# Another order of 879 operations in a transformer block on one core, with the last tile's output in 288 and 160 columns

## The chip, the cores and the metric

The kernel runs on one core of a Trainium2 chip. The metric is device microseconds of one execution. Beside it stands the profile of one further execution, whose span goes from the first to the last instruction. The engines are TensorE (PE; its weight loads are PEld), VectorE (DVE), ScalarE (ACT), GpSimd (POOL) and SyncE (SP), which here issues all DMA transfers.

## The reference

An attention layer with a sliding, dilated window, then a mixer and a two-layer product with gelu. S = 2048 rows, D = 448, F = 1792, 16 heads of 28, bf16.

```python
qkv = layernorm(x) @ wqkv                      # q, k, v
idx = pos[:, None] - arange(8) * 2             # 8 keys, every second row back
logits = einsum("bhsd,bhswd->bhsw", q, kg) * scale
p = softmax(where(mask, logits, -1e9)); o = einsum("bhsw,bhswd->bhsd", p, vg)
h = x + o @ wo
y = layernorm(h)
g = gelu(layernorm(y) @ w1)
x1 = y + shifted(g) @ w2                       # four column groups, shifted by 1 and 2 rows both ways
out = h + x1 + gelu(layernorm(x1) @ w3) @ w4
```

This is its shortened form; a layernorm subtracts the mean and divides by the square root of the variance plus 1e-5.

## The kernel before

All data stays in SBUF between the first load and the last store. The rows are worked in four stages t = 0 to 3 of 512 rows up to the hidden layer g, then in five units u = 0 to 4 of 2, 4, 4, 4 and 2 tiles of 128 rows. In the names below, the last digit is the stage or the unit.

- **N1, A1, V**: layernorm of x (N1), its turn into columns, the products for q and k (A1) and for v (V). Stages 0 and 1 are turned by TensorE with an identity, stages 2 and 3 by a DMA transpose from `lntm` to `actT`. V's results go to `vt`; DMA transfers copy them into windows, `vw` (four pieces a stage: vwp 16 rows of the stage before, vwa 64 rows, vwb 80 rows, vwc 16 rows of three tiles).
- **A2, S, A3, O**: VectorE multiplies q by shifted k (4096 elements a partition), TensorE sums the products with `zc`; the softmax (S); VectorE spreads the weights over `bd_r`, TensorE multiplies them with `vw` (A3: four groups of 32 small matmuls); O multiplies by wo and adds the residual.
- **B1, M**: layernorm of the sum and its DMA transpose (`actT`), product with w1 and gelu (M). B10 to B13 and M0 to M3 are its four stages. ACT's squares with running sums give the variance, ACT or POOL its power.
- **B2, T, W3, B3**, by unit: product of the shifted g with w2 (B2; from unit 2 on with rows gathered by small `ht` DMAs), layernorm and transpose (T), product with w3 and gelu to `h3T` (W3), product with w4, sum on VectorE and the output DMA (B3). Unit 4 is worked tile by tile.

A contraction of 448 is split over the upper and the lower 64 rows of TensorE: `duo` works two outputs as a **pair**, a first half (upper rows for one output, lower rows for the other) and a second half that swaps them and waits until the first is done.

What sets the order of the work is one list, `ORDER`, of 879 operation numbers. The phases are generated first, each operation with its number; `arrange` (line 192) then hands each engine its operations in the list's order, gives out the buffers of the pools in that order, and adds the waits. `OTHER` names the copies that go to their other engine (ACT to VectorE or back). A further rule stands in `arrange`: a DMA transpose waits for all loads and vw transfers ahead of it in the list, and those behind it wait for the transpose:

```python
if op.insts[0][0] == "dma_start_transpose":
    op.deps.update(turned + moved)
    turned, moved = [op], []
elif op.is_dma and not callable(op.chan):
    op.deps.update(turned)
    moved.append(op)
```

So the place of a load on SP decides which transposes it holds up and which hold it up. All instructions are recorded by one helper at line 1009 (1010 in the changed kernel), so that a profile's row is told apart by its tiles and shapes. Many copies from PSUM (`copy` in `phase_A1`, `phase_V`, the softmax and A3) may run on ACT or VectorE.

Of the kernel before, what the change touches and what calls it, by code (L numbers as in the profile page):

```python
# [15 lines left out]
NQK, NBD, NLN, NACT, NSM, NO = 3, 2, 2, 4, 1, 6  # L16
POWER = {'N1': 'aaaa', 'B1': 'aaaa', 'B2': 'apapp'}
RESIDUAL = 'ttvv'
ORDER = """
# [30 lines left out]
"""  # L50
OTHER = """
182 438 482 483 546 552
"""
FULL = (4,)
FILL = (0, 0, 0, 0)
# [226 lines left out]
def bass_sequential_preLN__sliding_local_dilated__mixer_s_mlp__prompt_kernel(  # L282
    nc, A_x, A_wqkv, A_wo, B_x, B_w1, B_w2, B_w3, B_w4, out,
):
    _, SEQ, D = A_x.shape
# [4 lines left out]
    NTL = SEQ // 128  # L290
# [22 lines left out]
    with ExitStack() as es:  # L313
# [87 lines left out]
        def dve(meth, block=False, **kw):  # L401
            op = S.add("dve", meth, **kw)
            op.block = block
            return op
# [4 lines left out]
        def dma(chan, out_ap, in_ap, nbytes, eng="sp", **kw):  # L409
            return S.add(eng, "dma_start", chan=chan, nbytes=nbytes, out=out_ap, in_=in_ap, **kw)  # L410
# [379 lines left out]
        def phase_A3(t):  # L790
# [14 lines left out]
            S.tag = "O%d" % t  # L805
            on_pe = RESIDUAL[t] == "t"
            summed = STATS["B1"][t] == "a"
# [59 lines left out]
        def phase_B2(u):  # L867
            tiles = UNITS[u]
            summed = STATS["B2"][u] == "a"
            dense = u >= 2  # L870
            n, first = 128 * len(tiles), 128 * tiles[0]
            if dense:
                for c, lo, hi, k, at in LOWER:
                    dma("ht", ht[at:at + hi - lo, k, 0:n], gT[lo:hi, c, 2 + first + SHIFT[c]:2 + first + SHIFT[c] + n], (hi - lo) * n * 2)

            def group(i, upper):
                b = _Tile(P_bank)

                def side(part, chunks):
                    return [(gT[part, c, 2 + i * 128 + SHIFT[c]:130 + i * 128 + SHIFT[c]], (lambda lo, m, c=c: w2_s[part, c, lo:lo + m])) for c in chunks]  # L880

                if dense:
                    top = side(TOP, range(3 + upper))
                    bot = [(ht[BOT, k, 128 * i - first:128 * i - first + 128], (lambda lo, m, k=k: w2_l[BOT, k, lo:lo + m])) for k in range(4 - upper)]
                else:
                    top, bot = side(TOP, range(4)), side(slice(64, KC), range(4))

                def out():
                    kw = dict(accum_out=mv[:, 2, i, 0:1]) if summed else {}
                    dve("scalar_tensor_tensor", out=xb[i], in0=xin[:, i, :], scalar=rs_y[:, 1, 0, i:i + 1], in1=b(lambda v: v[:, 0:D]), op0=ALU.mult, op1=ALU.add, **kw)  # L890
                    if not summed:
                        ln_stats(2, xb[i], i)

                return (lambda lo, n: b(lambda v: v[:, lo:lo + n]), top, bot), out

            for i in tiles[::2]:
                (A, out_a), (B, out_b) = group(i, True), group(i + 1, False)
                duo(A, B, ((0, D),))
                out_a()
                out_b()  # L900
            ln = _Tile(P_ln)
            if summed:
                sums_stats(2, tiles, lambda i: xb[i], ln)
            S.tag = "T%d" % u
            norms = norms_of("B2", u, len(tiles))
            rstd(2, tiles[0], len(tiles), summed, norms, POWER["B2"][u])
            last = [normalize(2, i, ln, n, xb[i], TURN["B2"][u], summed, norms[n]) for n, i in enumerate(tiles)]
            for i in tiles:
                S.add("pool", "tensor_tensor", after=last, out=xb[i], in0=xb[i], in1=xin[:, i, :], op=ALU.add).block = True
            b2_a[u] = transposed(ln, TURN["B2"][u], len(tiles))  # L910
# [20 lines left out]
        def phase_B3(u):  # L931
# [19 lines left out]
            else:  # L951
                for k, i in enumerate(UNITS[u]):
                    o = _Tile(P_o)
                    for n, (lo, m) in enumerate(((0, D // 2), (D // 2, D // 2)) if i == NTL - 1 else ((0, D),)):
                        b = _Tile(P_bank)
                        for first in range(0, NF, 7):
                            mms([(b(lambda v, m=m: v[:, 0:m]), h3[u][f](lambda v, k=k: v[:, k * 128:(k + 1) * 128]), w4_s[:, f, lo:lo + m],
                                  f == 0, f == NF - 1, m, None) for f in range(first, first + 7)])
                        store(i, b, o, lo, m, n)
# [27 lines left out]

        order = S.arrange([int(k) for k in ORDER.split()], [int(k) for k in OTHER.split()])
        _LAST["S"] = S; _LAST["order"] = order
# [61 lines left out]
```

## Time and profile before

| | us |
|---|---|
| median of 3 runs | 192.13 (191.79 to 192.33) |
| profiled execution | 191.2 |
| its span | 189.5 |
| TensorE busy | 180.3 |
| VectorE busy | 125.7 |
| ACT busy | 120.4 |
| POOL busy | 25.0 |

The span is the time from the first to the last instruction; the execution's own time is 1.7 us longer. TensorE's rows are matmuls, whose ends are modelled, so neighbours overlap. A releaser in brackets is what an engine waited for last.

### The profile page before, as it was taken

To read this page: it belongs to the slowest core of one execution; us is meant where nothing else is said; L and a number is where in the kernel's file an instruction comes from. 1 tells how busy PE (TensorE), PEld (TensorE's weight loads), DVE (VectorE), ACT (ScalarE), POOL (GpSimd) and SP (SyncE) were. 2 spreads that over 40 slices of the span, in tenths; PEclk is the share of its full clock that TensorE was granted. 3 is DMA by queue.
4 is the path that set the end of the run, shared out by engine and by line. 5 is a ranking of instruction groups with operands and counts; after the bars stand their busy time and mean duration, and the time that the engine had idled before them with its cause. 6 is when DMAs were issued, how large, how long until landed. Compare 5 with 4: busy or idle time off the path is not lost.

```text
span 189.5 us, 5776 instructions
## 1 busy us (share of the span) xinstructions
PE 180.3 (95%) x2496; PEld 93.8 (49%) x2496; DVE 125.7 (66%) x223; ACT 120.4 (64%) x289; POOL 25.0 (13%) x59
## 2 busy tenths in 40 slices
PE   6899998997999999999997999999999999999994
PEld 2474343443544574665444545554444544455773
DVE  6789899998999999989647437852086066000502
ACT  3659999887999999966794697232806004640250
POOL 3320000000000000244300000074002103900000
PEclk9999999999999999999999999999999999999999
DMA  5960045692654669902532210463300602300121
GB/s 133 362 207 0 9 93 138 162 203 46 127 125 90 129 201 378 249 13 38 147 71 50 58 35 3 96 76 91 118 24 7 114 0 73 83 0 0 52 73 48
DMA packets 33633, 18.59 MB, mean 98 GB/s; under 512 B 21336, under 2 KB 33096, under 8 KB 33608
## 3 DMA queue, kind: packets, MB, share of 16 engines
q1 hardware_dynamic: 33608, 18.23, 38.8%
q8 instruction: 19, 0.31, 0.7%
q14 instruction: 6, 0.05, 0.1%
HBM read 8.14 MB, written 1.84 MB: 53 GB/s over the span
## 4 chain that ended last, share of the span: by engine, by line
PE 66%; DMA 12%; DVE 10%; ACT 8%; POOL 1%; issue 1%; SPq 1%
PE ps L1009 66%; DMA actT<-lntm 5%; DMA vw<-vt 4%; ACT arena L1009 4%; DVE lntm L1009 3%; ACT actT L1009 2%; DVE st L1009 2%; DMA xin<-in_A_x_dram 2%; ACT lntm L1009 1%; POOL rs_y L1009 1%; DMA ht<-arena 1%; DVE arena L1009 1%; DVE qk_r L1009 1%; DVE xin L1009 1%; SPq L1009 1%
## 5 line engine op out<-in xcount | busy, mean ns | idle before, releaser
L1009 PE MATMUL ps<-actT,arena 64*128 64x512 bf16 (+2 forms) x812 | 70.4, 326 | 1.3 <-DMA actT<-lntm 0.6
L1009 ACT ACTIVATE h3T<-ps 128x512 bf16<-128x512 f32 (+1 forms) x70 | 30.5, 524 | 35.5 <-PE ps L1009 35.3
L1009 PEld LDWEIGHTS ps<-actT,arena 64*128 64x128 bf16 (+1 forms) x812 | 34.8, 96 | 33.0 <-PE ps L1009 1.7
L1009 PE MATMUL ps<-arena,h3T 64*128 64x448 bf16 (+2 forms) x434 | 44.5, 343 | 0.0
L1009 ACT ACTIVATE arena<-ps 128x512 bf16<-128x512 f32 (+6 forms) x64 | 29.5, 504 | 10.4 <-PE ps L1009 9.9
L1009 DVE SCALAR_TENSOR_TENSOR qk_r<-ps,mrs,arena 128x448 bf16<-128x448 f32 (+1 forms) x17 | 10.6, 651 | 33.9 <-PE ps L1009 18.5
L1009 DVE TENSOR_TENSOR qk_r<-arena 128x4096 bf16<-128x4096 bf16 (+1 forms) x16 | 31.9, 2014 | 0.7 <-PE ps L1009 0.7
L1009 PEld LDWEIGHTS ps<-arena,h3T 64*128 64x128 bf16 (+1 forms) x434 | 22.8, 94 | 19.2 <-ACT h3T L1009 0.2
L1009 POOL TENSOR_TENSOR arena<-arena,xin 128x448 f32<-128x448 f32 x16 | 16.2, 1033 | 54.2 <-DVE lntm L1009 38.5
L1009 DVE TENSOR_TENSOR bd_r<-arena,bmask 80x2048 bf16<-80x2048 bf16 x16 | 19.1, 1212 | 3.6 <-PE ps L1009 3.4
L1009 DVE SCALAR_TENSOR_TENSOR arena<-xin,rs_y,ps 128x448 f32<-128x448 bf16 x16 | 10.1, 674 | 8.5 <-PE ps L1009 8.5
L1009 ACT ACTIVATE actT<-ps 128x512 bf16<-128x512 f32 (+2 forms) x23 | 13.9, 636 | 2.1 <-PE ps L1009 1.9
L1009 PE MATMUL ps<-actT,w_s 64*112 64x512 bf16 x112 | 13.9, 379 | 1.3 <-DMA actT<-lntm 1.2
L1009 PE MATMUL ps<-wo_s,actT 64*128 64x448 bf16 x128 | 14.3, 350 | 0.4 <-ACT vt L1009 0.4
L1009 PE MATMUL ps<-arena,actT 64*128 64x448 bf16 x112 | 12.9, 350 | 0.1
L1009 PE MATMUL ps<-w_s,arena 64*128 64x448 bf16 x83 | 12.4, 349 | 0.5 <-DMA ht<-arena 0.5
L1009 ACT ACTIVATE lntm<-xin,nm 128x448 bf16<-128x448 bf16 x16 | 10.5, 658 | 2.1 <-DVE nm L1009 2.0
L1009 PEld LDWEIGHTS ps<-actT,w_s 64*112 64x112 bf16 x112 | 7.6, 126 | 6.2 <-DVE bd_r L1009 1.7
L1009 ACT ACTIVATE rs_x<-mv,epsilon 128x4 f32<-128x4 f32 (+2 forms) x16 | 4.4, 292 | 9.3 <-DVE mv L1009 9.2
L1009 DVE BATCH_NORM_STATS2 st<-xin 128x6 f32<-128x448 bf16 x16 | 9.0, 614 | 1.1 <-DMA xin<-in_A_x_dram 1.0
L1009 DVE TENSOR_SCALAR lntm<-arena,mv,rs_y 128x512 bf16<-128x512 f32 x14 | 6.8, 543 | 3.5 <-POOL rs_y L1009 2.9
L1009 PEld LDWEIGHTS ps<-w_s,arena 64*128 64x128 bf16 x83 | 5.7, 95 | 6.3 <-DMA ht<-arena 1.2
(72 smaller groups left out, 157.9 us busy)
## 6 DMA issues: line engine op xcount, KB each, us to landing
arena<-in_B_w_dram SPq DMA_DIRECT2D x2, 896.0 KB, 7.1
out_dram<-qk_r SPq DMA_DIRECT2D x15, 112.0 KB, 1.8
arena<-in_B_w_dram SPq DMA_DIRECT2D x2, 784.0 KB, 8.9
vw<-vt SPq DMA_DIRECT2D x4, 320.0 KB, 3.8
vw<-vt SPq DMA_DIRECT2D x4, 256.0 KB, 6.3
arena<-in_A_wqkv_dram SPq DMA_DIRECT2D x2, 448.0 KB, 4.5
xin<-in_A_x_dram SPq DMA_DIRECT2D x2, 448.0 KB, 7.0
xin<-in_A_x_dram SPq DMA_DIRECT2D x3, 224.0 KB, 5.3
```

What stands on the lines that cost most here:

```text
L1009: inst = getattr(eng, meth)(**kw)
```

## The change

`ORDER` is another list. `OTHER` goes from {182, 438, 482, 483, 546, 552} to {92, 182, 483, 489, 492, 495, 546, 552}: the copies 92 (A1 of stage 0) and 489, 492, 495 (A3 of stage 3) go from ACT to VectorE, 438 (A1 of stage 3) and 482 (softmax of stage 3) go back to ACT. `DENSE` names the unit from which `ht` is used, 2 as before. The last tile's output is worked in 288 and 160 columns, not 224 and 224.

```diff
+DENSE = 2
 ORDER = """
-2 0 8 1 29 7 9 11 39 10 40 33 12 13 36 14 15 16 30 17 18 41 19 42 31 43 32 50 55 56 20 51 6 52 62 37 44 45 57 58 53 60
...
+8 9 2 10 12 0 1 39 40 41 42 43 44 45 46 47 48 49 13 5 14 4 15 16 6 33 7 50 17 18 29 51 36 37 34 30 52 55 53 54 56 62
...
 OTHER = """
-182 438 482 483 546 552
+92 182 483 489 492 495 546 552
 """
...
-            dense = u >= 2
+            dense = u >= DENSE
...
-                    for n, (lo, m) in enumerate(((0, D // 2), (D // 2, D // 2)) if i == NTL - 1 else ((0, D),)):
+                    for n, (lo, m) in enumerate(((0, 288), (288, 160)) if i == NTL - 1 else ((0, D),)):
```

SP in the first quarter, before: behind the loads of x and wqkv, from wo's second load to the second DMA transpose (A13). `wo_s` is wo, `w_s` is w1 (two halves) and w2; the first four vw pieces after the first transpose are V0's and one of V1.

```order
L1009 DMA_TRANSPOSE actT<-lntm 128x16x128
L1009 DMA wo_s<-in_A_wo_dram 28x4x448 x2
L1009 DMA vw<-vt 80x4x512
L1009 DMA vw<-vt 64x4x512
L1009 DMA vw<-vt 16x3x512 x2
L1009 DMA wo_s<-in_A_wo_dram 28x4x448
L1009 DMA w_s<-in_B_w_dram 128x2x448 x2
L1009 DMA w_s<-in_B_w_dram 112x4x448
L1009 DMA vw<-vt 80x4x512
L1009 DMA vw<-vt 64x4x512
L1009 DMA_TRANSPOSE actT<-lntm 128x16x128
```

The same place after, up to the second transpose; `arena` from `in_B_w` 128x2x1792 is the first half of w3.

```order
L1010 DMA wo_s<-in_A_wo_dram 28x4x448 x4
L1010 DMA w_s<-in_B_w_dram 128x2x448 x2
L1010 DMA w_s<-in_B_w_dram 112x4x448
L1010 DMA_TRANSPOSE actT<-lntm 128x16x128
L1010 DMA vw<-vt 80x4x512
L1010 DMA vw<-vt 16x3x512
L1010 DMA vw<-vt 64x4x512
L1010 DMA vw<-vt 16x512
L1010 DMA vw<-vt 64x4x512
L1010 DMA vw<-vt 16x3x512
L1010 DMA vw<-vt 80x4x512
L1010 DMA arena<-in_B_w_dram 128x2x1792
```

The weights wo, w1 and w2 moved ahead of the first transpose, the vw pieces of V0 and V1 follow it without a load between them, and half of w3 stands ahead of the second transpose.

SP a little later, before: the pieces of V2 behind the second transpose (A13), the transposes of B10 and B11, then w3 and the first piece of V3.

```order
L1009 DMA vw<-vt 64x4x512
L1009 DMA vw<-vt 16x3x512
L1009 DMA vw<-vt 80x4x512
L1009 DMA vw<-vt 16x512
L1009 DMA_TRANSPOSE actT<-lntm 128x16x128 x2
L1009 DMA arena<-in_B_w_dram 128x2x1792 x2
L1009 DMA vw<-vt 16x512
```

The same place after:

```order
L1010 DMA vw<-vt 80x4x512
L1010 DMA vw<-vt 64x4x512
L1010 DMA vw<-vt 16x512
L1010 DMA_TRANSPOSE actT<-lntm 128x16x128 x2
L1010 DMA arena<-in_B_w_dram 128x2x1792
L1010 DMA vw<-vt 16x3x512
```

V2's piece of 16 rows of three tiles moved behind both transposes and behind the second half of w3.

TensorE from the end of O2 to M2, before. `wo_s` is O2, `arena,h3T` is B30 (the product with w4), `actT,arena` of 512 columns is W31, `ident,pb` the turn of the softmax's weights, `actT,w_s` M2 and `bd_r,vw` A33.

```order
L1009 MATMUL ps<-wo_s,actT 128x448 x8
L1009 MATMUL ps<-arena,h3T 128x448 x14
L1009 MATMUL ps<-wo_s,actT 128x448 x8
L1009 MATMUL ps<-arena,h3T 128x448 x28
L1009 MATMUL ps<-actT,arena 128x512 x58
L1009 MATMUL ps<-ident,pb 80x64 x16
L1009 MATMUL ps<-actT,arena 128x512 x20
L1009 MATMUL ps<-actT,w_s 112x512 x22
```

The same place after:

```order
L1010 MATMUL ps<-wo_s,actT 128x448 x8
L1010 MATMUL ps<-arena,h3T 128x448 x56
L1010 MATMUL ps<-actT,arena 128x512 x38
L1010 MATMUL ps<-ident,pb 80x64 x16
L1010 MATMUL ps<-actT,arena 128x512 x18
L1010 MATMUL ps<-actT,w_s 112x512 x22
L1010 MATMUL ps<-bd_r,vw 32x64 x64
L1010 MATMUL ps<-actT,w_s 112x512 x6
```

The whole of O2 now stands ahead of B30, and 22 of W31's matmuls moved from ahead of M2 to behind it.

58 rows, old and new, of the table ORDER are left out of this document.

## The prediction

> **What bounds the kernel now.** I read four things in this order: the page's totals and slices, the busy time by stretch, the list of what each engine waited for, and the chain of work that ended last. First the totals and the forty slices of the span:
>
> ```profile
> PE 180.3 (95%) x2496; PEld 93.8 (49%) x2496; DVE 125.7 (66%) x223; ACT 120.4 (64%) x289; POOL 25.0 (13%) x59
> PE   6899998997999999999997999999999999999994
> DVE  6789899998999999989647437852086066000502
> PEclk9999999999999999999999999999999999999999
> DMA  5960045692654669902532210463300602300121
> ```
>
> TensorE is busy 180.3 of 189.5 us, at the full granted clock in every slice. Its last 17 slices hold no gap, so whatever can be won lies earlier. VectorE's 66% is an average that hides the point: it is full up to slice 17 and half idle later. Busy time by stretch (us, then busy time and instructions of PE, PEld, DVE, ACT, POOL) says it in numbers:
>
> ```profile
> 8.12:130.00 121.88, 117.47 (x1871) 60.93 (x1873) 101.78 (x169) 96.61 (x236) 15.15 (x36) 1.00 0.47 113
> 130.00:186.67 56.67, 56.67 (x601) 30.42 (x596) 17.62 (x37) 19.85 (x44) 7.75 (x8) 1.00 0.19 49
> 13.00:85.00 72.00, 69.38 (x1181) 34.64 (x1181) 69.14 (x94) 66.47 (x170) 3.20 (x4) 1.00 0.52 129
> ```
>
> From 130 us on TensorE is busy 56.67 of 56.67. From 8.12 us (its first matmul with data) to 130 it is idle 121.88 - 117.47 = 4.4 us. From 13 to 85 us VectorE is busy 69.14 of 72.00, as full as TensorE (69.38): a stall taken from TensorE there is only worth what VectorE can follow. The waits of TensorE:
>
> ```profile
> PE ps L1009 <- DMA actT<-lntm: 1.8, 2, 1.2
> PE ps L1009 <- DMA vw<-vt: 1.0, 1, 1.0
> PE ps L1009 <- DMA ht<-arena: 0.5, 1, 0.5
> PE ps L1009 <- ACT vt L1009: 0.4, 1, 0.4
> ```
>
> These four are 3.7 of the 4.4 us. The timeline of TensorE has each of them, with the idle time and its releaser in brackets:
>
> ```profile
> 29.59 1.27 PE L1009 MATMUL ps<-actT,arena 64*128 64x512 bf16 x12 [0.64 <-DMA actT<-lntm]
> 42.52 0.74 PE L1009 MATMUL ps<-wo_s,actT 64*128 64x448 bf16 x6 [0.41 <-ACT vt L1009]
> 46.02 0.42 PE L1009 MATMUL ps<-bd_r,vw 80*32 80x64 bf16 x32 [0.99 <-DMA vw<-vt]
> 102.74 1.07 PE L1009 MATMUL ps<-actT,w_s 64*112 64x512 bf16 x8 [1.20 <-DMA actT<-lntm]
> 113.12 0.36 PE L1009 MATMUL ps<-w_s,arena 64*128 64x448 bf16 x1 [0.46 <-DMA ht<-arena]
> ```
>
> The chain (start, duration, what) shows what stood behind them:
>
> ```profile
> 25.10 4.35 DMA actT<-lntm
> ...
> 37.73 8.25 DMA vw<-vt
> ...
> 46.02 31.07 PE ps L1009 x506
> ...
> 77.11 0.42 DVE actT L1009
> ...
> 83.03 1.94 POOL rs_y L1009
> ...
> 91.89 2.73 ACT lntm L1009 x8
> ...
> 95.25 1.38 DVE lntm L1009 x4
> ...
> 96.66 5.94 DMA actT<-lntm
> ...
> 102.74 6.31 PE ps L1009 x170
> ...
> 126.14 60.81 PE ps L1009 x636
> ...
> 186.97 0.45 DVE qk_r L1009
> ```
>
> From 77 to 97 us the end is set by VectorE, POOL and ACT (layernorm B12), then by the transpose that M2 waits for. So M2's first matmul, 102.74 us, is the gate to everything behind it.
>
> **The change, part by part.** TensorE's own work is the same (2496 matmuls of the same shapes but for the last tile), so the sum is over waits.
>
> (a) The loads of wo, w1 and w2 leave before the first DMA transpose instead of behind it, with no vw transfer queued behind them. In before the vw of V1 waited behind w1 and w2 and took 8.25 us; the vw transfers of this trace in all:
>
> ```profile
> L1009 SPq DMA_DIRECT2D vw<-vt x15: 627/690/2394, 19.5 to 102.6; - x15
> DMA to landing us min/median/max: 2.2/3.9/8.5
> ```
>
> With the median 3.9 us the vw of V1, issued by about 35 us, is there by 39, seven us before it is wanted at 46: the wait of 0.99 goes. What hides the loads, issued from 7 us on behind x, is the stretch of 14 to 24 us: the DMA row has 0 in slices 3 and 4. If that cover were gone, the transpose of A12, which waits for every load ahead of it, would be late by what is left of them. The wait for ACT's vt copy (0.41) falls to about 0.1, since O0 stands later. The transpose of A12 is issued after the same normalizations, about 25.1, and TensorE has 0.65 us more to do before it needs it: 0.64 becomes 0.2 to 0.4. Sum of (a): -0.99 - 0.3 - 0.3 = -1.6.
>
> (b) Some halves of a pair now stand side by side. The second half of a pair waits until the first is done; such neighbours start 0.1 to 0.25 us later than the usual step (the chain breaks at one of them, the pair of M3, at 126.14). Before W31 there are six instead of four, behind M2 two instead of one: +0.3 and +0.15.
>
> By (a) and (b) TensorE would come to M2 1.3 us less late. But that is only TensorE's side.
>
> (c) The gate, M2. On TensorE, 22 of W31's matmuls move from ahead of M2 to behind it. This row gives their price:
>
> ```profile
> L1009 PE MATMUL ps<-actT,arena 64*128 64x512 bf16 x420 | 49.4, 377 | 0.9 <-DMA actT<-lntm 0.6
> ```
>
> 49.4 / 420 = 0.118 us each is 2.6 us; started one behind the other they overlap a little, and I take 2.4. So M2 must start 2.4 us earlier only to break even. When it can start is set on VectorE. Adding up VectorE's durations of before in the new order, 1.3 us less work stands ahead of the last normalization of B12, the new copy in A1 of stage 0 (0.6 us) counted in. That copy and a small reduction that is moved fall into two waits of VectorE before 12 us, which gives back 0.9. Against it: ACT's squares and square roots of B12 (2.73 + 0.6 us in the chain) now have only one operation of VectorE of 0.6 beside them, 0.7 less than before. Net 96.66 - 1.3 - 0.9 + 0.7 = 95.2 for the issue of the transpose, if VectorE keeps the waits that it has now:
>
> ```profile
> DVE bd_r L1009 <- PE ps L1009: 0.8, 1, 0.8
> DVE qk_r L1009 <- PE ps L1009: 0.7, 1, 0.7
> DVE actT L1009 <- PE ps L1009: 0.2, 1, 0.2
> ```
>
> These are all it waited from 13 to 85 us, 1.7 us, each for TensorE. If all go, the issue is at 93.5; I take half: 94.3. Then the transpose's own time. The ten of this trace:
>
> ```profile
> DMA to landing us min/median/max: 3.1/4.3/5.9
> ```
>
> The longest is this very one, 5.94; the nearest row of the same form is 4.35. With 4.35 it lands at 98.65 and M2 starts at 98.8, 3.95 earlier than 102.74. Less 2.4: a gain of 1.55. TensorE alone would have reached M2 at about 97.4, so a wait of 1.2 us or so stays there.
>
> (d) Behind M2: the ht transfers are issued earlier against their use (0.46 becomes 0.15 at most), neighbours +0.15, and the pair of M3 that stands side by side in before is parted (-0.2): -0.4. The copies of A33 that go to VectorE, 489, 492 and 495, fall into its idle time (28.75 busy of 45.00 from 85 to 130 us):
>
> ```profile
> 85.00:130.00 45.00, 43.22 (x612) 22.17 (x612) 28.75 (x63) 27.76 (x61) 9.49 (x13) 1.00 0.35 66
> ```
>
> If that cover were gone they would cost 3 x 0.6.
>
> (e) The last tile. Its last sum on VectorE covers 160 columns, not 224:
>
> ```profile
> L1009 DVE SCALAR_TENSOR_TENSOR qk_r<-ps,mrs,arena 128x448 bf16<-128x448 f32 x15 | 9.7, 677 | 27.7 <-issue 15.4 <-PE ps L1009 12.2
> L1009 DVE SCALAR_TENSOR_TENSOR qk_r<-ps,mrs,arena 128x224 bf16<-128x224 f32 x2 | 0.9, 451 | 6.2 <-PE ps L1009 6.2
> ```
>
> (677 - 451) / 224 = 1.0 ns a column, so 64 columns are 0.06 us; a shorter output transfer gives nothing to 0.05: -0.1. TensorE's 448 columns in all are the same.
>
> Sum: -1.55 - 0.4 - 0.1 = -2.05, rounded up for the waits of which I counted the smaller end: -2.2. The profiled execution took 191.2 us (span 189.5 and 1.7 around it), so 189.0; it stands 0.93 below the median of 192.13, so **189.9**.
>
> One rule bears on the 5.94 us. The trace shows one packet of 16 KB on queue 8 inside that transpose (at 100.59 us, 0.93 us long, on one DMA engine that still had transpose packets to move); the page counts the queue:
>
> ```profile
> q8 instruction: 19, 0.31, 0.7%
> ```
>
> The Trainium skill, "Runtime: NRT & Kernel Launch", section "Instruction fetch mechanics", says that a sequencer fetches its instructions in 16 KiB blocks by a DMA queue of its own, and that crossing a block is mostly hidden. By that rule the transpose would be as fast as the others wherever it stands, and the time the one above; this trace shows a transpose 1.6 us longer with such a packet in it, and others untouched (one of 4.36 has one as well).
>
> **The rivals.**
> 1. *The transpose of B12 meets a fetch again.* TensorE's place in its program at that time is such that its next block of instructions is due at about 95 to 97 us, within the transpose's 94.3 to 98.7. For it: 5.94 in before. Against: nine of ten were not hit. Price 5.94 - 4.35 = 1.6: 191.5.
> 2. *VectorE follows wholly*: its 1.7 us of waits all go and the issue is at 93.5: 0.8 less, 189.1.
> 3. *VectorE does not follow*, because its products come later than the matmuls that need them; the issue stays at 95.2 or later and with rival 1's price nothing is left: 189.9 + 0.9 + 1.6 = 192.4, no change.
> 4. *Slower: vw of V2 behind half of w3.* Its 48 KB piece for the windows' first rows now stands behind the second load of w3 (896 KB), issued at about 66. A32's second group wants it at 71.5 to 72.
>
> ```profile
> arena<-in_B_w_dram SPq DMA_DIRECT2D x2, 896.0 KB, 7.1
> ```
>
> Two such loads together took 7.1; one alone should be through the queues in about half, so I expect the piece at 70 to 71.5 and no stall. If it took the 8.5 us at the end of the vw row above, it would land at 75, stall TensorE, and the whole layernorm chain behind O2, by 3 us: 192.9. It decides from a latency of 8.2 us on; below 5.5 it costs nothing.
>
> The order does do what it says: the SP and PE rows are moved as told, so a change without effect is no case.
>
> **How the numbers follow.** Forecast 189.9 (189.2 to 190.7) 0.45; rival 1, 191.5, 0.24; rival 2, 189.1, 0.10; rival 3, 192.4, 0.10; rival 4 or another new wait of that size, 0.11. Within 0.3% (about what a measurement of this kernel can tell from no change) is 191.55 to 192.71. Faster: 0.45 + 0.10 + half of rival 1 (0.12) + a little of rival 3 = 0.68. Same: 0.12 + 0.08 = 0.20. Slower: 0.12. The range, 188.7 to 192.3, leaves out rival 4 and the far ends.
>
> **What would show it.** Right: no wait of PE for vw or vt at 35 to 48 us; VectorE still about 96% busy from 13 to 85; a transpose issued near 94 with M2's matmuls behind it, waiting about 1 us; PE full from 130 on. Rival 1 shows as a transpose of about 5.9 there, rival 4 as a wait for vw near 72, rival 3 as an issue after 95. The prediction is wrong if TensorE waits for an engine where it did not before, above all for ACT (66.47 of 72.00 busy from 13 to 85), of which I assumed that it keeps up.

## The result, and the profile after

The changed kernel takes 189.97 us (median of 10 runs, 188.16 to 190.5) against 192.12 for before (10 runs): a ratio of 0.9892, 95% interval 0.9854 to 0.9931. A second set of runs gave 190.26 (12 runs, 189.33 to 191.55) against 191.44, ratio 0.9944 (0.9914 to 0.9973). So it is faster by 0.6 to 1.1%, and its single executions lie further apart than either gain. Some executions were disturbed and ran longer, most of them at a granted clock of 0.98 to 0.99; the ratios and the medians leave them out, but for the 192.12, which holds two (193.37 and 195.54).

That spread is half of the story, so two profiled executions of the changed kernel are read here side by side. The first took 188.16 us (span 186.4) and was its fastest run; the one of the second set took 191.55 (span 189.8) and was the longest of that set. First the slices and the busy time by stretch of the first one:

```profile
PE   6899998999999999999999999999999999999994
DVE  6799999999999999999476587614087274000403
```

```profile
13.00:85.00 72.00, 70.87 (x1253) 35.98 (x1251) 71.61 (x102) 67.08 (x171) 3.06 (x3) 1.00 0.57 133
85.00:130.00 45.00, 44.66 (x566) 22.57 (x564) 27.66 (x58) 29.98 (x63) 8.57 (x12) 1.00 0.35 63
```

From slice 7 on TensorE's row is full but for the last. VectorE went from 69.14 to 71.61 of 72.00 us busy between 13 and 85 us: it has no wait left there in this execution. TensorE's idle time from 85 to 130 fell from 1.8 to 0.3 us. What TensorE waited for, in whole:

```profile
PE ps L1010 <- POOL mhalf L1010: 1.6, 1, 1.6
PE ps L1010 <- DMA actT<-lntm: 0.5, 1, 0.5
PE ps L1010 <- DVE lntm L1010: 0.5, 1, 0.5
```

The first and the last lie ahead of the first matmul with data. Of the four waits of before only A12's transpose is left, 0.5 us. M2, the gate of the prediction, started without a wait:

```profile
96.64 1.02 PE L1010 MATMUL ps<-actT,arena 64*128 64x512 bf16 x7
97.48 1.26 PE L1010 MATMUL ps<-actT,w_s 64*112 64x512 bf16 x10
```

W31 runs into M2 with no bracket behind either row; the transpose was issued at 92.90 and landed at 97.19, 4.29 us later:

```profile
L1010 SPq DMA_TRANSPOSE actT<-lntm x1: 1820/1820/1820, 92.9 to 92.9; - x1
...
DMA to landing us min/median/max: 4.3/4.3/4.3
```

From M2's start to the end of the span it was 88.9 us, against 86.8 before. The last tile ends as forecast:

```profile
184.00 0.38 DVE L1010 SCALAR_TENSOR_TENSOR qk_r<-ps,mrs,arena 128x160 bf16<-128x160 f32 x1 [0.29 <-PE ps L1010]
```

The second execution, same program, has these waits of TensorE behind its first matmuls:

```profile
PE ps L1010 <- DMA vw<-vt: 1.0, 1, 1.0
PE ps L1010 <- issue: 0.9, 1, 0.9
...
PE ps L1010 <- DVE arena L1010: 0.5, 1, 0.5
PE ps L1010 <- DMA ht<-arena: 0.4, 1, 0.4
```

And where they are, by TensorE's timeline:

```profile
43.55 0.41 PE L1010 MATMUL ps<-bd_r,vw 80*32 80x64 bf16 x29
44.87 0.21 PE L1010 MATMUL ps<-bd_r,vw 80*32 80x64 bf16 x3 [0.92 <-issue]
...
73.82 0.42 PE L1010 MATMUL ps<-bd_r,vw 80*32 80x64 bf16 x32 [0.50 <-DVE arena L1010]
...
103.09 0.68 PE L1010 MATMUL ps<-bd_r,vw 80*32 80x64 bf16 x63 [0.96 <-DMA vw<-vt]
...
112.03 0.36 PE L1010 MATMUL ps<-w_s,arena 64*128 64x448 bf16 x1 [0.43 <-DMA ht<-arena]
```

The first is a stop inside one group of 32 matmuls, after 29 of them, with no semaphore to wait for (releaser "issue"); what it waited for is taken up behind the experiments. The second names VectorE, whose row ended about when V2's small vw piece landed, at 73.68, 6.18 us after its issue; the first execution had it at 71.16, in time. The third is V3's piece of 16 rows, issued behind the transpose of B12. Together 2.8 of the 3.4 us between the two executions.

### The profile page after: what moved, and what is told of

The parts are those of the page before. It is cut to its first block, busy times and chain, and to the rows that moved or that the text cites. A ratio compares the mean times of both kernels' runs of the same rounds, so it can differ in the third digit from the quotient of the medians.

```text
span 186.4 us, 5772 instructions
## 1 busy us (share of the span) xinstructions
PE 180.3 (97%) x2496; PEld 94.0 (50%) x2496; DVE 127.0 (68%) x225; ACT 122.1 (65%) x289; POOL 24.0 (13%) x59
## 4 chain that ended last, share of the span: by engine, by line
PE 79%; DVE 14%; ACT 4%; DMA 1%; issue 0%; SPq 0%
PE ps L1010 79%; DVE qk_r L1010 9%; DVE st L1010 1%; ACT lntm L1010 1%; DMA xin<-in_A_x_dram 1%; DVE lntm L1010 1%; ACT L1010 1%; DVE mx L1010 1%; DVE xin L1010 1%; ACT arena L1010 1%; ACT h3T L1010 1%; DVE pb L1010 0%; DVE ls L1010 0%; DVE mv L1010 0%; ACT rs_x L1010 0%
## 5 line engine op out<-in xcount | busy, mean ns | idle before, releaser
L1010 PEld LDWEIGHTS ps<-actT,arena 64*128 64x128 bf16 (+1 forms) x812 | 35.4, 96 | 31.9 <-PE ps L1010 1.9
L1010 PE MATMUL ps<-arena,h3T 64*128 64x448 bf16 (+3 forms) x434 | 44.9, 343 | 0.2
L1010 ACT ACTIVATE arena<-ps 128x512 bf16<-128x512 f32 (+6 forms) x66 | 30.7, 508 | 8.5 <-PE ps L1010 8.1
L1010 DVE SCALAR_TENSOR_TENSOR qk_r<-ps,mrs,arena 128x448 bf16<-128x448 f32 (+2 forms) x17 | 10.4, 651 | 30.9 <-PE ps L1010 30.9
L1010 PE MATMUL ps<-actT,w_s 64*112 64x512 bf16 x112 | 13.4, 379 | 0.0
L1010 PE MATMUL ps<-arena,actT 64*128 64x448 bf16 x112 | 12.3, 351 | 0.2
L1010 ACT ACTIVATE actT<-ps 128x512 bf16<-128x512 f32 (+2 forms) x19 | 11.7, 639 | 1.1 <-PE ps L1010 1.0
L1010 ACT ACTIVATE vt<-ps 128x448 bf16<-128x448 f32 x16 | 8.3, 546 | 0.5 <-PE ps L1010 0.5
```

The lines of the kernel that those rows point to most:

```text
L1010: inst = getattr(eng, meth)(**kw)
```

## The experiments

Kernels were run in four sets, each on a chip of its own, and all ratios are against before on the same chip. The changed kernel to set them against has the medians 189.97 and 190.26 and the ratios 0.9892 and 0.9944. These two ratios differ by half a per cent, so that differences of that size from the changed kernel are not certain, and differences in us are across chips, but for the late loads.

**The changed kernel again.** No edit.

> The changed kernel once more, for a second profile and for comparison on this chip: 1.1% faster than before, 189.5 to 190.5 us by the median. Theory: the gap between the earlier profiled execution (188.16) and the median comes from DMA transposes that meet an instruction fetch in some executions, so the time of a single execution may again lie anywhere from 188 to 190.5.

190.26 us, profile as above. The spread is there, and its place was misjudged: no wait for a transpose grew (A12's 0.5 is all), the four stalls above did.

**The early loads alone, on before.**

```diff
@@ SP of before @@
-wo1 wo2 | V0 vwb vwa vwc, V1 vwc | wo3 w1a w1b w2 | V1 vwb vwa     (all behind the transpose of A12)
+wo1 wo2 wo3 w1a w1b w2 | transpose of A12 | V0 vwb vwa vwc, V1 vwc vwb vwa
```

> Before, with the loads of wo, w1 and w2 ahead of the first DMA transpose and nothing else. Theory (the loads carry the gain up to layernorm B12, and VectorE follows): the wait of 0.99 us for vw at 46 us is gone, VectorE's wait of 0.8 us right behind it too, M2's transpose is issued about 0.8 to 1.0 us earlier, and the time falls by 0.7 to 1.1 us. Rival (VectorE is the bound from 13 to 85 us and does not follow): the wait for vw goes, the wait for M2's transpose grows by as much, and the time falls by less than 0.3.

191.45 us, ratio 1.0022 (0.9993 to 1.0051): no gain. But the rival is not what its profile shows either. The wait for vw is gone from TensorE's list, M2's transpose is issued at 95.43 in place of 96.66, and M2 starts 1.26 us earlier:

```profile
101.48 1.29 PE L1009 MATMUL ps<-actT,w_s 64*112 64x512 bf16 x10 [1.17 <-DMA actT<-lntm]
...
129.08 1.26 PE L1009 MATMUL ps<-actT,arena 64*128 64x512 bf16 x10 [0.89 <-DMA actT<-lntm]
```

VectorE followed, and the time was lost again at W32, where before had no wait: the transpose of T2 (second row's releaser) was issued at 122.98, 1.5 us earlier than in before, and landed only 0.5 earlier. It took 5.96, that of B12 5.91:

```profile
95.43 5.91 DMA actT<-lntm
...
122.98 5.96 DMA actT<-lntm
```

**The late loads, on the changed kernel.**

```diff
@@ SP of the changed kernel @@
-wo1 wo2 wo3 w1a w1b w2 | transpose of A12 | V0 vwb vwc vwa, V1 vwp vwa vwc vwb | w3a
+transpose of A12 | wo1 wo2 | V0 vwb vwc vwa, V1 vwp | wo3 w1a w1b w2 | V1 vwa vwc vwb | w3a
```

> The changed kernel with the loads of wo, w1 and w2 back behind the first DMA transpose, at the places that they had in before. Theory: V1's pieces of vw are late by 4 us or more, TensorE waits for them between 40 and 48 us for 1 to 3 us, and the time rises by 0.7 to 2.5. Rival (the order of the products carries the gain): less than 0.3.

192.3 us, ratio 1.0048 (1.0008 to 1.0088), 2.0 us slower than the changed kernel on this chip, within the expected 0.7 to 2.5. The wait came at another place than the one named: not A31's vw but A13, whose transpose now waited for w3a behind all of it.

```profile
39.30 8.18 DMA arena<-in_B_w_dram
47.50 5.94 DMA actT<-lntm
```

```profile
53.57 0.61 PE L1010 MATMUL ps<-actT,arena 64*128 64x512 bf16 x4 [2.44 <-DMA actT<-lntm]
```

So the new order can't do without the early loads. The loads can't do without the new order either.

**The instruction fetches moved, on before.** The 42 matmuls of the q and k pairs of A12 become 84 of half the columns. The computation is the same.

```diff
-    for h, out, (lhsT, rhs) in ((0, out_u, upper[k]), (1, out_l, lower[k])):
-        specs.append((h, dict(out=out(lo, m), lhsT=lhsT, rhs=rhs(lo, m), ...
+    for lo2, m2 in ((lo, m // 2), (lo + m // 2, m // 2)) if S.tag in SPLIT else ((lo, m),):
+        for h, out, (lhsT, rhs) in ((0, out_u, upper[k]), (1, out_l, lower[k])):
+            specs.append((h, dict(out=out(lo2, m2), lhsT=lhsT, rhs=rhs(lo2, m2), ...
```

> Before, with the 42 matmuls of the q and k pairs of stage 2 each split into two of half the columns: the same work in 84 more TensorE and weight-load instructions, so that every later instruction fetch of TensorE comes about 84 instructions earlier. Theory (the fetch inside the transpose of B12 makes it 5.94): the fetch falls ahead of the transpose's packets, the transpose takes 4.3 to 4.5, the wait at M2 falls from 1.2 to 0.2 or less, and the time falls by 0.5 to 1.2 us if the split itself costs nothing. Rival (something else at that place makes it long, as the transfers beside it): it takes 5.5 to 6 again.

190.8 us, ratio 0.9976 (0.9944 to 1.0008): not told apart from nothing. The transpose did as expected: no fetch falls into that of B12 any more, it takes 4.3 us, and M2 no longer waits 1.2.

```profile
L1011 SPq DMA_TRANSPOSE actT<-lntm x1: 1881/1881/1881, 98.0 to 98.0; - x1
...
DMA to landing us min/median/max: 4.3/4.3/4.3
```

The profiled execution lost the same elsewhere. TensorE stood still for 1.87 us at 43.81, inside a group as above, and waited 1.4 for ht:

```profile
41.55 0.39 PE L1011 MATMUL ps<-bd_r,vw 80*32 80x64 bf16 x27
43.81 0.23 PE L1011 MATMUL ps<-bd_r,vw 80*32 80x64 bf16 x5 [1.87 <-issue]
```

**Both on before**: the early loads and the moved fetches.

> Before, with the early loads of wo, w1 and w2 and the 42 matmuls of stage 2's q and k pairs split in two, both at once. Alone the early loads took the wait for vw away and changed nothing in the time: their profile shows the transposes of B12 and T2 at 5.9 us, each with an instruction fetch late in it, and M2 and W32 waiting 1.2 and 1.0 us for them. Alone the split moved the fetches out of both. Theory (it is the fetches in these two transposes that took the gain of the loads): both transposes take 4.3 to 4.6, their waits are gone, and the time falls by 1.0 to 2.2 us against before. Rival (VectorE's chain is the gate whatever the transposes take): less than 0.5.

191.2 us, ratio 0.9996 (0.9968 to 1.0025). My theory fell. The transposes of B12 (4.30) and T2 (4.38) were short as expected, and the time is where it was. The fetches now fall into the transposes of B11 (5.31) and B13 (5.39), and TensorE waits at M1 and for ht:

```profile
66.90 1.47 PE L1011 MATMUL ps<-actT,w_s 64*112 64x512 bf16 x11 [0.95 <-DMA actT<-lntm]
...
112.16 0.36 PE L1011 MATMUL ps<-w_s,arena 64*128 64x448 bf16 x1 [1.11 <-DMA ht<-arena]
```

In the order of before, the chain of VectorE, transpose and next product arrives at M1, M2, B22 and W32 with hardly any slack in turn, and in these runs what was won ahead of one was lost at the next. The new order has slack there: M2 and W32 wait in none of its nine profiles, M1 in one (the copies below) and B22 in one (0.43, above).

**VectorE 2 us fuller, on the changed kernel.** A maximum over four tiles of x into a scratch tile, read by nobody.

```diff
+    S.ops[363].insts = [("tensor_reduce", dict(out=scr[:, 0:4], in_=xin[:, 8:12, :], axis=AX.X, op=ALU.max))] + S.ops[363].insts
```

> The changed kernel with one more operation on VectorE, a maximum over four tiles of x into a scratch tile that nobody reads, ahead of the second product of A2 of stage 2 (near 50 us): 1.8 to 2.0 us more for VectorE and nothing else. Theory (VectorE is as full as TensorE from 13 to 85 us, 71.6 of 72.0 busy): it comes out at the end by 1.0 to 2.0 us. Rival (TensorE alone bounds, VectorE has slack): 0 to 0.4.

191.73 us (191.03 to 192.44), ratio 1.0017 (0.9992 to 1.0042): 1.5 us slower than the changed kernel. The operation took 2.00 us. TensorE now waits for a product:

```profile
PE ps L1012 <- DVE qk_r L1012: 1.2, 1, 1.2
```

**ScalarE 2.1 us fuller, on the changed kernel.** Four copies of 384 columns into a scratch tile, read by nobody.

```diff
+    for n, k in enumerate((153, 156, 159, 162)):
+        S.ops[k].insts = [("activation", dict(out=scr[:, n, :], in_=xin[:, 12 + n, 0:384], func=ACT.Copy))] + S.ops[k].insts
```

> The changed kernel with four more copies on ScalarE, 384 columns of x each into a scratch tile that nobody reads, one ahead of each copy of A3 of stage 0 (near 38 to 45 us): 2.3 to 2.5 us more for ScalarE and nothing else. Theory (ScalarE has 4 to 6 us of slack from 13 to 85 us, VectorE none): 0 to 1 us, since the four copies themselves come 0.6 us later each. Rival (ScalarE is as full as VectorE): 1.5 to 2.5 us.

190.62 us (189.62 to 192.43), ratio 0.9965 (0.9933 to 0.9997): 0.4 us slower than 190.26, with an interval that overlaps that of the second set. The four copies took 2.1 us in all, 0.52 each. So ScalarE has slack for most of it, where 2.0 us more on VectorE came out as 1.5.

**The copies on their old engines, in the new order.**

```diff
-92 182 483 489 492 495 546 552
+182 438 482 483 546 552
```

> The changed kernel's order with the copies on the engines of before (92, 489, 492 and 495 on ScalarE, 438 and 482 on VectorE). Theory: 438 (0.6 us) falls into VectorE's full stretch and 92 leaves it before 12 us, where VectorE has waits; the gate at M2 is 0 to 0.6 us later, and A33's three copies on ScalarE make O3 later by up to 1 us: 0.2 to 1.2 us slower than the changed kernel. Rival (the copies are free on either engine): within 0.3 us of it.

191.66 us (190.65 to 193.47), ratio 1.0024 (0.999 to 1.0058): 1.4 us slower than the changed kernel, so without the moved copies the new order gains nothing. In its profile the transpose of B11 is issued 1 us after that of B10 has landed (63.11 against 62.07), where both profiles of the changed kernel have 0.07. From there everything behind is late: M1 waits, then the second load of w3 and V2's piece behind it.

```profile
67.51 0.85 PE L1010 MATMUL ps<-actT,w_s 64*112 64x512 bf16 x6 [0.48 <-DMA actT<-lntm]
...
74.73 0.42 PE L1010 MATMUL ps<-bd_r,vw 80*32 80x64 bf16 x32 [1.23 <-DMA vw<-vt]
```

It also has the stop inside a group of A3:

```profile
44.21 0.21 PE L1010 MATMUL ps<-bd_r,vw 80*32 80x64 bf16 x2 [0.54 <-issue]
```

That 438's 0.6 us on VectorE is the one that does it fits the place (stage 3's A13, just ahead of that layernorm); the six copies were not tried one by one.

**The split of the last tile alone, on before.** `(0, 224), (224, 224)` becomes `(0, 288), (288, 160)`.

> Before, with the last tile's output in 288 and 160 columns and nothing else. Both theories: 0.05 to 0.15 us less, which a measurement of this kernel can't tell from nothing; the profile shows the last sum on VectorE at about 0.38 to 0.40 us in place of 0.45, and the last transfer at 1.5 us as before.

191.21 us, ratio 0.9987 (0.9952 to 1.0021): no difference that can be told, as expected. The last sum takes 0.38 us, as in the row of the changed kernel above. The profiled execution, the longest of its set (195.63), has a stop inside a group of A3 too:

```profile
47.27 0.35 PE L1009 MATMUL ps<-bd_r,vw 80*32 80x64 bf16 x23 [3.25 <-issue]
```

**Two vw pieces earlier, on the changed kernel.**

```diff
@@ SP of the changed kernel @@
-V2 vwb vwa vwp | transposes of B10, B11 | w3b | V2 vwc | w2's rows | V3 vwa vwb | w4 | V3 vwc | w4 | transposes of T1, B12 | V3 vwp
+V2 vwb vwa vwp vwc | transposes of B10, B11 | w3b | w2's rows | V3 vwp vwa vwb | w4 | V3 vwc | w4 | transposes of T1, B12
```

> The changed kernel with two vw pieces issued earlier: V2's piece of three tiles before the transposes of B10 and B11 instead of behind the second half of w3, and V3's piece of 16 rows before the other pieces of V3 instead of behind the transpose of B12. Theory: in the second profile of the changed kernel these two landed late and cost TensorE 0.7 and 1.0 us, in the first they cost nothing, so the typical execution falls by 0.5 to 1.5 us, to 188.8 to 189.8. Rival (what these waits cost is taken back at the next gate, M2's or W32's transpose): within 0.3 us of the changed kernel.

189.11 us (188.12 to 189.63, 6 runs), ratio 0.9866 (0.9822 to 0.991): 1.15 us faster than the changed kernel's 190.26, and clear of its second interval (0.9914 to 0.9973) though not of its first (0.9854 to 0.9931). The two waits for vw are gone; the stop for instructions is still there in its profile:

```profile
PE ps L1010 <- issue: 1.3, 1, 1.3
```

**Half of w3 earlier, on the changed kernel**: w3a goes from 35 us, ahead of A13's transpose, to 11 us, behind w2.

```diff
@@ SP of the changed kernel @@
-w1a w1b w2 | transpose of A12 | V0, V1 vw | w3a | transpose of A13
+w1a w1b w2 w3a | transpose of A12 | V0, V1 vw | transpose of A13
```

> The changed kernel with the first half of w3 ahead of the first DMA transpose, behind w1 and w2, instead of at 35 us. Theory: in three of four profiles of the changed order TensorE stood still for 0.5 to 1.3 us inside one group of A3 near 44 us, with no semaphore to wait for; its fetch of instructions came about 2 us later than in the fast profile, while half of w3 (896 KB) was in the queues. Without it there the fetch is on time, that stall is gone, and the typical execution falls by 0.6 to 1.3 us, to 189.0 to 189.7. Against it: the load may still be under way when the transpose of A12 is ready at 25.5 us, which would cost up to 1 us there. Rival (the stall has another cause, or another wait takes its place): within 0.3 us of the changed kernel.

189.17 us (188.78 to 190.14, 7 runs), ratio 0.9901 (0.9867 to 0.9935): 1.1 us faster than 190.26 by the median, but the interval overlaps both of the changed kernel's, so this run alone does not settle it. Its profile has no stop for instructions; A12's transpose was not held up (issued at 25.59, in the changed kernel at 25.53). The wait for V3's piece is there, as in the second profile; the page names ScalarE for it:

```profile
PE ps L1010 <- ACT arena L1010: 0.7, 1, 0.7
PE ps L1010 <- DMA actT<-lntm: 0.6, 1, 0.6
```

**Both moves on the changed kernel.**

> Both moves together: the two vw pieces earlier and the first half of w3 ahead of the first DMA transpose. Theory (the two are separate stalls): the gains add, 187.6 to 188.6 us. Rival (both were paid out of the same slack ahead of M2 or W32): 188.8 to 189.3, as with the vw pieces alone.

188.38 us (188.19 to 190.78, five of six runs at or below 188.47), ratio 0.9872 (0.9823 to 0.9921). By the median it is 1.9 us below the changed kernel's 190.26 and 2.8 below before on its chip (191.21); by the ratios it is 1.4 below the second set and 0.4 below the first. Five of its six executions took 188.47 or less, and of the changed kernel's 22 only one did. Its interval overlaps those of the two single moves, so that the gains add is not shown. It is the fastest kernel of this study by its median. Its profile has TensorE waiting for nothing but A12's transpose, as in the first execution of the changed kernel:

```profile
PE ps L1010 <- POOL mhalf L1010: 1.6, 1, 1.6
PE ps L1010 <- DMA actT<-lntm: 0.5, 1, 0.5
```

## Why the prediction was right, and which steps were not

The forecast of 189.9 met the median of 189.97, and the gate at M2 did open by a gain on VectorE, as forecast. That the figure met so closely is luck: one term was too small by 1.3 us, and stalls that the sum has no term for took about as much back.

(a) *The waits for vw and vt go.* Right at the places named: neither is left at 35 to 48 us in either profile. A12's wait became 0.49 and 0.51, not 0.2 to 0.4. But I read the loads as carrying the gain. The runs show them to be necessary (2.0 us without them) and worth nothing alone (1.0022).

(b) *Neighbouring halves.* No run took this apart; it stays an estimate.

(c) *The gate at M2.* This step was mis-sized. I let VectorE keep half of its 1.7 us of waits, with an issue at 94.3 and a wait of 1.2 at M2. In the first profile VectorE kept none (71.61 of 72.00), the issue was at 92.90, earlier than the earliest end I had worked out (93.5), and M2 started at 97.48 with no wait, 1.3 us earlier than the 98.8 of the sum. This is rival 2, which I gave 0.10.

A likely reason why the issue came earlier still: the list of waits shows 1.7 us, but VectorE's idle time in that row of before is 72.00 - 69.14 = 2.86, and after it is 0.39; no run takes this apart. My 97.4 for TensorE alone was also loose, since 102.74 - 1.20 - 1.3 - 2.4 gives 97.8. In the second profile, late by then from other stalls, VectorE waited 1.4 us for TensorE, the issue was at 94.99 and M2 had no wait either. The reading behind the step, that VectorE is as full as TensorE, is borne out by the extra 2.0 us on VectorE that came out as 1.5.

Rival 1's fetch did come: a packet of 16 KB began at 96.65, 3.74 us after the issue. It cost nothing there, for the transpose took 4.29. And nine of ten not hit in before was misread: T2's transpose, with a packet 0.80 us after its issue, took 4.93.

(d) *Behind M2.* From M2 to the end the first profile took 2.2 us more than before, where the terms add up to 2.4 - 0.4 - 0.1 = 1.9. The ht wait was gone in one execution and 0.43 in the other, against 0.15 at most. I looked at 489, 492 and 495, which fall into idle time and show no cost, and not at 438, which left a full engine. Putting all six back costs 1.4 us.

(e) *The last tile.* 0.45 became 0.38, as forecast; in the time it can't be told.

With (c) alone corrected, the forecast would have been 189.9 - 1.3 = 188.6, 1.4 us under the median. The profiles of slower executions show what fills the gap: the stop for instructions (0.92), V2's piece behind w3 (0.50), V3's piece behind B12's transpose (0.96) and ht (0.43). V2's piece is rival 4: I expected half of w3 to be through in half of 7.1 us, and it took 5.31 and 6.38 in the two profiles, the piece behind it 5.11 and 6.18, short of the 8.2 from which it would have decided. The run with both moves bears out that these stalls are costs of the change: three transfers in better places take 1.9 us off by the median, 1.4 by the ratios of the second set. With them the same order of products is 2.8 us below before on its chip, and the change as it was made got 1.2 (191.44 to 190.26) or 2.15 (192.12 to 189.97).

On the fetches, the Trainium skill, "Runtime: NRT & Kernel Launch", section "Instruction fetch mechanics", calls the crossing of a 16 KiB block mostly hidden. For most crossings the traces agree. Not for one near 43 us: TensorE stopped there for 0.92, 1.27 and 0.54 us in three profiles of the new order, and for 1.87 and 3.25 in two of the old (the split matmuls and the last tile alone). In all five exactly 1217 of its instructions are on record ahead of the stop, though the orders differ and the groups stop after 27, 29, 30 or 9 matmuls. So it is a place in the stream of instructions, and not a tile, that TensorE waited at. Here the measurement decides.

The traces show what the load has to do with it. TensorE was 256 instructions ahead of that place (about one packet's worth: 19 packets go with some 5000) at 38.7 to 39.2 us in the eight profiles of the new order with the early loads. With half of w3 moved away the next packet began 0.3 and 0.6 us later, with it at its place 1.4 to 3.8 us later (six profiles). The packet came at 42.04 to 42.56 in the three that stopped and by 41.68 in the three that did not. So, by these eight executions, the load delays the packet, and the stop follows when the packet is late enough. The load is not the only thing that does: in the run of the early loads alone on before, where no load was under way, the packet began 2.3 us behind that place.

## What to carry to other kernels

Where two engines are both full over a long stretch, a wait removed on one is worth what the other can follow, and what the next gates have in slack: check each gate behind it, and test by filling an engine on purpose. A small transfer that somebody waits for belongs ahead of a large load on the same queue: V2's piece of 48 KB landed 5.1 to 6.8 us after its issue behind half of w3 (six profiles), 2.6 and 2.8 us when it was issued ahead of it. And one profile is one execution: two profiles of the same program told the stall that both have (A12's 0.5) from those that only one has, and the latter were cheap to remove.

## What the runs showed of the hardware

The time of a DMA transpose of 128x16x128 depended on TensorE's instruction fetch. In 13 traces of this study (nine such transposes each) 65 had no 16 KB packet of queue 8 begin in the first 4.3 us after their issue, and all of them took 4.25 to 4.44 us. The 52 that had one took 4.26 to 6.00. By the time from the issue to the packet: 4.5 to 5.4 us with the packet 0.4 to 1.3 us after the issue (one at 0.14 took 4.29), 5.15 to 5.4 at 2.0 to 2.15, 5.5 to 5.7 at 2.4 to 3.2, and from 3.7 on nearly all or nothing: six took 5.9 to 6.0, at 3.85 to 4.01, the others 4.3 to 4.6. What is late in these six is the end alone: in before's transpose of B12 the 2048 packets of 256 bytes were done by 100.60, the 16 KB packet ran from 100.59 to 101.52, and the last two of the transpose's 32 packets of 4 bytes began only at 101.51 and 101.52; the other five show the same. Any change in the count of TensorE's instructions, or in its pace, moves the packets against the transposes, so an order with no slack behind its transposes can gain and lose 1 to 1.6 us at a transpose by chance; in the two runs with split matmuls B12's went from 5.94 to 4.29 and 4.30, and B11's from 4.27 to 4.91 and 5.31.
